# Retention attention by chunks of 64 positions on four array quarters, for the units of the last two batch groups

## The chip, the cores and the metric

One Trainium2 chip, one core. The time is device microseconds of one execution, the median of several; lower is better. Everything is float32 on the array.

## The reference

```python
def _attn_ref(q, k, v):                    # each (8, 8, 576, 64): batch, heads, positions, head_dim
    scores = (1 / sqrt(64)) * q @ k^T
    gamma = 1.0 - 2.0 ** (-5.0 - arange(H))
    Dmat = where(rel >= 0, gamma ** rel, 0)         # rel = query position - key position
    return (scores * Dmat) @ v

def _moe_ref(x, w1, w2, w3, w_out):        # x: (4608, 512), w1, w2: (512, 1024), w3: (1024, 1024), w_out: (1024, 512)
    return (((x @ w1) * (x @ w2)) @ w3) @ w_out

def reference(...):
    x = attention.transpose(0, 2, 1, 3).reshape(4608, 512)
    return _moe_ref(x, ...)
```

The decay factors as gamma^i * gamma^-j, so the kernel scales q rows by gamma^i / 8 and v rows by gamma^-j, masks the scores with a triangle of ones, and carries a state: the sum of k^T v over all earlier positions.

## The kernel before

**Attention in units.** Two batches at a time (four such pairs, i) and five chunks of the 576 positions (c): a unit g = 5 i + c, 20 in all. The first chunk of a pair has 64 positions, the other four have 128. A unit does, for two batches and eight heads:

- `score(g)` (line 233): k times q, 16 matmuls with 64 contraction rows and 128 output rows; DVE multiplies the four banks with the triangle into `pm` (line 236).
- `state(g)` (line 255): adds k^T v of the unit to the PSUM bank `st`; ACT copies it to `sb` (line 259) for the next unit. The last chunk of a pair has none.
- `pv_state(g)` (line 274): `sb` times q, 16 matmuls of 64 x 64, one on each quarter of the array in turn, into two banks `xps`.
- `pv(g)` (line 299): v times `pm`, added to the same banks; ACT copies them to `xT` (line 306), the token blocks.

Each f32 matmul shows as two records in the profile, each a weight load and a matmul.

**Two phases.** Up to about 366 us the program converts the weights, multiplies w3 and w_out together, and handles the first half of the tokens with one level of Strassen's scheme (`up`, `down`). From there on (units 10 to 19, `for g in range(2 * NC, G)`), tokens go in four groups with two levels of Strassen's scheme in the first product. One group is 17 items, done in order by `work(n)` from the list `todo`:

- 14 items `up2` (line 1028): seven small products each, with weight forms `ra` that are fetched from HBM by `next_forms` (line 939) into a ring of three slots. An `up2` takes PSUM tiles `p1` and `p5` from the pool `acc` and `p6` from `seed`. Its last product (`rest`: `A22`, `-T4`) is put off into the next item by way of `behind` and run by `finish()`. Sums lie on DVE (lines 1038, 1040), POOL (`more`, line 1033) and ACT (lines 1042 to 1057); `multiply()` makes the gated product `ab` on DVE (line 1003).
- 3 items `down` (line 637): seven products of 128 x 256 over `ab`, results to `ot`, stored by ACT's queue.

`token_forms(gr)` (line 948) makes a group's sums on POOL from `xT`: `E` and its fourth form `E4` (first-level sums of both token blocks) and `T`, `U` (second level).

**Order around a unit.** The order is written out by hand, each engine running its instructions in program order. `dealt` says how many items go to each unit. Between the items, `scale_blocks` (POOL) and `front_blocks` (DVE transposes) get q and k of the next unit ready, `front` (transposes on TensorE) k of units 11 to 13, `scale` (ACT) its v. The lists `aside`, `beside` and `loads` hold small steps that an item takes up at fixed points. Then, between two items and in one go: `pv(g)`, in a group's last unit (13, 16, 19: `ready`) `finish()` and `multiply()`, then the loads for g + 2 on POOL's queue, `state(g + 1)`, `score(g + 1)`:

```python
        pv(g)()
        if g in ready:
            finish()
            multiply()
        if g + 2 < G:
            load(g + 2, "v", nc.gpsimd)
            ...
        if g + 1 < G:
            state(g + 1)
            score(g + 1)
```

[...] In the second phase they are one for `st`, five for `acc`, two for `seed` (`open_second`).

Of the kernel before, what the change touches and what calls it, by code (L numbers as in the profile page):

```python
# [8 lines left out]
F32 = mybir.dt.float32  # L9
# [5 lines left out]
PSUM = bass.MemoryType.PSUM  # L15
# [4 lines left out]
def kernel(  # L20
# [30 lines left out]
    starts = [0] + [short + c * P for c in range(NC - 1)]  # L51
    G = NB2 * NC
    NB = 3
    TB = S // NB
# [23 lines left out]
    open_attention(att_part)  # L78
    st_ps = ctx.enter_context(tc.tile_pool(name="st_ps", bufs=1, space=PSUM))
    acc_part = ExitStack()  # L80
    acc = acc_part.enter_context(tc.tile_pool(name="acc", bufs=7, space=PSUM))

# [3 lines left out]

    def load(g, names, engine=nc.sync):
        i, c = divmod(g, NC)
        sz = sizes[c]
        src = {"k": k, "q": q, "v": v}  # L90
        for nm in names:
            t = pools["ld"].tile([P, 2 * H, D], F32, tag="ld_" + nm, name="ld_" + nm)
            engine.dma_start(
                t[:sz], src[nm][2 * i:2 * i + 2, :, starts[c]:starts[c] + sz, :].rearrange("b h p d -> p (b h) d"))
            live[nm, g] = t
# [181 lines left out]

    def pv(g):

        if ("xps", g) not in live:  # L280
            pv_state(g)
        i, c = divmod(g, NC)
        sz = sizes[c]
        live["x", g] = True
        vs, pm, banks = live["v", g], live["pm", g], live["xps", g]

        parts = []
        for n in range(NB):
            lo, hi = max(starts[c], n * TB), min(starts[c] + sz, (n + 1) * TB)
            if lo < hi:  # L290
                m = i * NB + n
                if ("xT", m) not in live:
                    live["xT", m] = xps[m % 4 == 3].tile([P, NP, 2, TB], F32, tag="xT", name="xT")
                parts.append((live["xT", m], lo - n * TB, lo - starts[c], hi - lo))
        for m, (b, n) in enumerate(bank_order):
            for r in range(2):
                for half in range(2):
                    p, j = 2 * r + n, half ^ r
                    nc.tensor.matmul(banks[r][heads[half], b, n, :sz], vs[:sz, b * H + 2 * p + j, :],  # L299
                                     pm[:sz, b, j, p, :sz], start=(c == 0 and m == 0), stop=True,  # L300
                                     skip_group_check=True)

        def evict():
            for x, to, fr, n in parts:
                for r in range(2):
                    nc.scalar.copy(
                        x[:, 2 * r:2 * r + 2, :, to:to + n].rearrange("p n b s -> p b n s"),
                        banks[r][:, :, :, fr:fr + n])

        return evict  # L310

    blocks = [(("A", r, f), None) for f in range(2) for r in range(2)]
# [309 lines left out]
    def down(x, y, then=None, last=False):  # L625
# [34 lines left out]

        C11, C12, C21, C22 = (0, 0), (0, 1), (1, 0), (1, 1)
        product(1, "A11", "B11")
        first = ot[:, 0, 0]
# [4 lines left out]
        if second:  # L668
            store()
            finish()  # L670
        product(7, "S3", "T3")
        if second:
# [8 lines left out]
        nc.vector.tensor_add(ot[:, 0, 1], ps[6], first)  # L681
        nc.scalar.copy(ot[:, 0, 0], ps[2])
        early = second or last or g >= 2 * NC - 1
        if early:
# [8 lines left out]
        if second:  # L693
            store()
        product(3, "S4", "B22", on=5)
        while aside and not early:
# [10 lines left out]
    def store():  # L707
        while stores:

            nc.scalar.dma_start(*stores.pop(0))  # L710
# [210 lines left out]
    def open_second():  # L921
        nonlocal acc
        flush()
        acc_part.close()
        acc = ctx.enter_context(tc.tile_pool(name="acc", bufs=5, space=PSUM, reuse_waits="tile"))
        pools["seed"] = ctx.enter_context(tc.tile_pool(name="seed", bufs=2, space=PSUM, reuse_waits="tile"))
        ra = wp.tile([P, 32 * P], F32, tag="wA1", name="ra")
        cs = wp.tile([P, 2, 4, 2, TB], F32, tag="wS1", name="cc")
        ring.extend([ra[:, :FORM], ra[:, FORM:2 * FORM]])
        free.extend(cs[:, j] for j in range(2))  # L930
        live["first"] = [ra[:, 2 * FORM + j * DM // 2:2 * FORM + (j + 1) * DM // 2] for j in range(2)]
        for _ in range(2):
            next_forms(nc.sync)
# [8 lines left out]
    def token_forms(gr):  # L942
# [13 lines left out]
        sums += [(T[:, s, 2], x[s][:, 2:, 0], T[:, s, 1]) for s in range(2)]  # L956
        for args in sums:
            tt(*args)
        tt(b12, b22, b12)
# [14 lines left out]
        if gr:  # L974
            rest()
        tt(T[:, 1, :, 0], T[:, 1, :, 1], T[:, 1, :, 0])
        for k in (slice(0, 2), 2):
# [13 lines left out]
    def finish():  # L991
        while behind:
            behind.pop(0)()
# [14 lines left out]
    def up2(gr, n):  # L1008
# [26 lines left out]
        def plus(ps, j, with_add=None):  # L1035
# [5 lines left out]
            else:  # L1041
                nc.scalar.copy(c[:, j], ps)

        p1 = acc.tile([P, 2, TB], F32, tag="acc", name="up")
        product(p1, "A11", "B11", True)
# [4 lines left out]
        product(p5, "S1", "T1", True)  # L1050
        nc.scalar.copy(c[:, 3], p5)  # L1051
        finish()
        next_forms()
        if loads:
# [9 lines left out]
        product(p1, "A12", "B21")  # L1064
        plus(p1, 0, add)
        product(p5, "S4", "B22")
        if add is not None:
# [11 lines left out]
        if aside:  # L1079
            aside.pop(0)()  # L1080

        def rest():
# [108 lines left out]
    load_blocks(g + 1, "q")  # L1191
    state(g)
    score(g)
    add_group(0)
    dealt = [3, 4, 4, 3, 3, 7, 7, 3, 7, 7]
    for g in range(2 * NC, G):
        n = dealt[g - 2 * NC]
        if g + 1 < G:
            beside.extend(lambda j=j: scale(g + 1, "v", range(j, j + H // 2)) for j in (0, H // 2))
            tail = min(n, 4) - 3  # L1200
# [4 lines left out]
            for nm in "qk":  # L1205
                blocks_in = nm == "q" or g + 1 not in whole
                if blocks_in:
                    aside.append(lambda nm=nm: front_blocks(g + 1, nm))
                work(1)
                while aside:  # L1210
                    aside.pop(0)()
                if not blocks_in:
                    while loads:
                        loads.pop(0)()
                    front(g + 1, "k")
                if g + 2 < G and not (nm == "k" and g + 2 in whole):
                    load_blocks(g + 2, nm)
            work(tail)
            for left in (loads, beside):
                while left:  # L1220
                    left.pop(0)()
        else:
            work(n)
        pv(g)()
        if g in ready:
            finish()
            multiply()
        if g + 2 < G:
            load(g + 2, "v", nc.gpsimd)
            if (g + 2) % NC != NC - 1:  # L1230
                loads.append(lambda g=g: load(g + 2, "k", nc.gpsimd))
        if g + 1 < G:
            state(g + 1)
            score(g + 1)
        if g in ready:
            add_group(ready[g])
        if g == G - 1:
            token_forms(ready[g])
    g = G
# [44 lines left out]
```

## Time and profile before

| | |
|---|---|
| median of 3 runs | 850.87 us (846.77 to 853.91) |
| the profiled execution's own time | 850.68 us |
| its span, first to last instruction | 848.9 us |
| granted TensorE clock, mean | 0.989 |
| PE busy | 819.3 us (97%), 6085 matmul records |
| DVE, ACT, POOL busy | 541.2, 283.2, 325.6 us |

PE is TensorE's matmuls, PEld its weight loads, DVE VectorE, ACT ScalarE, POOL GpSimd, SP SyncE's queue. A row of the timeline has the start, the length from the first start to the last end, engine, line, what is written and read, the array rows and columns used, the moving operand's shape and the number of records; in brackets the idle time ahead of it and what ended it. The ends of matmuls are modelled and overlap the next ones, so a rate is read from the starts of successive rows.

### The profile page before, as it was taken

What the parts mean: (1) busy time and instruction counts of PE and PEld (TensorE: products, weight loads), DVE (VectorE), ACT (ScalarE), POOL (GpSimd) and SP (SyncE); (2) the same over time, 40 slices, a digit from 0 to 9 for tenths busy, and PEclk for the clock granted to TensorE, in tenths of its full rate; (3) what the DMA queues carried; (4) which work ended last, traced back from release to release, by engine and by line L of the source; (5) the groups of instructions that cost most, each with busy time, mean ns of one, the idle gap of its engine ahead of it and who ended that gap; (6) DMA issues with size and microseconds to landing.
All of it is one profiled execution on the core that took longest, in us unless ns stands there. A gap on an engine that the chain in (4) does not pass through costs nothing.

```text
span 848.9 us, 15774 instructions
## 1 busy us (share of the span) xinstructions
PE 819.3 (97%) x6085; PEld 738.1 (87%) x6085; DVE 541.2 (64%) x887; ACT 283.2 (33%) x581; POOL 325.6 (38%) x330
## 2 busy tenths in 40 slices
PE   7899999999999999979998999999999999999998
PEld 6889999644989998869998889998899998899987
DVE  4899999991644477615657644759735768446653
ACT  4777556670111101033343024342034331033300
POOL 1100010001104181395545935556916468445500
PEclk8999999999999999999999999999999999999999
DMA  9995454436046487979786147787275452245401
GB/s 193 217 224 128 77 150 125 126 98 112 1 98 125 75 220 251 307 209 220 190 229 167 44 93 228 201 238 177 58 156 183 140 208 69 77 148 189 159 25 51
DMA packets 201291, 126.96 MB, mean 150 GB/s; under 512 B 161272, under 2 KB 183032, under 8 KB 201216
## 3 DMA queue, kind: packets, MB, share of 16 engines
q1 hardware_dynamic: 170944, 50.14, 29.1%
q0 software_dynamic: 11776, 63.71, 23.0%
q10 hardware_dynamic: 18496, 12.10, 5.3%
q8 instruction: 48, 0.79, 0.4%
q14 instruction: 27, 0.22, 0.1%
HBM read 103.62 MB, written 22.28 MB: 148 GB/s over the span
## 4 chain that ended last, share of the span: by engine, by line
PE 79%; DMA 7%; DVE 7%; issue 3%; SPq 2%; ACT 1%; POOL 0%; ACTq 0%; DVEq 0%; POOLq 0%
PE po L637 24%; PE up L1028 15%; PE up L524 13%; PE seed L1028 11%; PE ps L477 6%; DMA ld_v<-in_v_dram 3%; PE xps L299 3%; PE sc L233 3%; DMA ra<-kept 2%; PE xps L274 1%; SPq L171 1%; DVE c L529 1%; DVE ab L1003 1%; DMA bl_q<-in_q_dram 1%; PE st L255 1%
## 5 line engine op out<-in xcount | busy, mean ns | idle before, releaser
L637 PE MATMUL po<-w3o,ab 128*128 128x256 f32 x552 | 125.0, 381 | 1.4 <-DVE ot L641 0.5
L637 PEld LDWEIGHTS po<-w3o,ab 128*128 128x128 f32 x552 | 103.9, 190 | 17.4 <-DVE ot L641 1.2
L1033 POOL TENSOR_TENSOR cc<-cc 128x384 f32<-128x384 f32 x112 | 109.3, 1001 | 4.1 <-ACT cc L1051 2.4
L1040 DVE TENSOR_TENSOR cc<-seed,cc 128x384 f32<-128x384 f32 x88 | 48.7, 553 | 72.9 <-PE seed L1028 68.5
L181 POOL TENSOR_TENSOR bl_q<-bl_q,gqs 128x512 f32<-128x512 f32 (+1 forms) x30 | 30.8, 1048 | 127.7 <-DMA bl_q<-in_q_dram 91.8
L939 POOL DMA_DIRECT2D ra<-kept x54 | 30.6, 567 | 124.1 <-PE seed L1028 103.3
L1028 PE MATMUL up<-xT,ra 128*128 128x192 f32 x384 | 74.2, 330 | 0.6 <-DMA ra<-kept 0.6
L1040 DVE TENSOR_TENSOR cc<-up,cc 128x384 f32<-128x384 f32 x88 | 48.4, 550 | 36.8 <-PE up L1028 31.5
L524 PE MATMUL up<-xT,wA 128*128 128x192 f32 x384 | 70.4, 327 | 0.0
L529 DVE TENSOR_TENSOR c<-up,c 128x384 f32<-128x384 f32 x80 | 44.0, 550 | 38.9 <-PE up L524 38.3
L1028 PEld LDWEIGHTS up<-xT,ra 128*128 128x128 f32 x384 | 64.4, 192 | 2.0 <-DMA ra<-kept 0.9
L236 DVE TENSOR_TENSOR pm<-sc,mask 128x512 f32<-128x512 f32 (+1 forms) x80 | 45.4, 626 | 32.1 <-PE sc L233 32.0
L637 PE MATMUL po<-wB,forms 128*128 128x256 f32 x288 | 65.2, 379 | 0.5 <-DVE forms L611 0.5
L524 PEld LDWEIGHTS up<-xT,wA 128*128 128x128 f32 x384 | 63.4, 190 | 1.1 <-issue 0.5
L637 PEld LDWEIGHTS po<-wB,forms 128*128 128x128 f32 x288 | 54.6, 190 | 8.2 <-PE po L637 0.8
L1047 ACT COPY seed<-up 128x384 f32<-128x384 f32 x56 | 25.9, 463 | 100.1 <-PE up L1028 46.6
L1028 PE MATMUL seed<-e,ra 128*128 128x192 f32 x256 | 52.9, 337 | 5.2 <-DVE cc L1040 2.9
L1028 PE MATMUL up<-ra 128*128 128x192 f32 x288 | 55.1, 328 | 1.9 <-DMA ra<-kept 1.9
L477 PE MATMUL ps<-wo,w3T 128*128 128x512 f32 x128 | 55.1, 592 | 0.0
L204 POOL TENSOR_TENSOR ld_v<-ld_v,gk 128x1024 f32<-128x1024 f32 (+1 forms) x9 | 17.1, 1899 | 90.5 <-DMA ld_v<-in_v_dram 90.5
L679 DVE TENSOR_TENSOR ab<-ab,forms 128x512 f32<-128x512 f32 x17 | 17.1, 1008 | 53.3 <-PE po L637 53.3
L1028 PEld LDWEIGHTS seed<-e,ra 128*128 128x128 f32 x256 | 43.7, 194 | 7.8 <-DVE cc L1040 3.6
(127 smaller groups left out, 1597.2 us busy)
## 6 DMA issues: line engine op xcount, KB each, us to landing
ra<-kept POOLq DMA_DIRECT2D x54, 896.0 KB, 5.0
raw<-in_moe_w_dram SPq DMA_DIRECT2D x72, 128.0 KB, 3.0
bl_q<-in_q_dram SPq DMA_DIRECT2D x216, 32.0 KB, 3.2
out_dram<-ot ACTq DMA_DIRECT2D x54, 128.0 KB, 2.3
bl_k<-in_k_dram SPq DMA_DIRECT2D x136, 32.0 KB, 2.4
raw<-in_moe_w_dram SPq DMA_DIRECT2D x16, 256.0 KB, 6.0
ld_k<-in_k_dram SPq DMA_DIRECT2D x8, 512.0 KB, 5.9
raw<-in_moe_w_out_dram SPq DMA_DIRECT2D x32, 128.0 KB, 2.7
```

Source lines behind the costliest of these rows:

```text
L181: nc.gpsimd.tensor_tensor(out=part, in0=part, in1=gqs[:, :, n0:n0 + n].unsqueeze(3).to_broadcast([P, NP, n, BL]), op=ALU.mult)
L233: nc.tensor.matmul(sc[j][:sz, p, :sz], kT[hs, b, p, :sz], qT[hs, b, p, :sz], start=True, stop=True)
L236: nc.vector.tensor_mul(pm[:sz, b, j, :, :sz], sc[j][:sz, :, :sz], mask[:sz, :sz].unsqueeze(1).to_broadcast([sz, NP, sz]))
L477: nc.tensor.matmul(ps, live["w3T", ft][:, g, :], live["wo"][:, g, :], start=(g == 0), stop=(g == KF - 1))
L524: nc.tensor.matmul(ps[:, w, :], a[:, w, r, :], b[:, r, :], start=(new and w == r == 0), stop=(w == r == 1), skip_group_check=True)
L529: nc.vector.tensor_add(c[:, to], ps, c[:, sb])
L637: nc.tensor.matmul(ps[nm], a[A][:, f, :], live["W"][B][:, f, :], start=(f == 0 and not on), stop=(f == NP - 1), skip_group_check=True)
L939: engine.dma_start(ring[n % 3], kept[n % 14 // 7][nm])
L1028: nc.tensor.matmul(ps[:, w, :], weight_of(slot, a, w), B[b], start=(new and w == 0), stop=True, skip_group_check=True)
L1033: nc.gpsimd.tensor_tensor(out=o, in0=o, in1=i, op=ALU.add)
L1040: nc.vector.tensor_add(c[:, j], ps, with_add[:, j])
L1047: nc.scalar.copy(p6, p1)
```

## The change

For the units of the second phase, 10 to 19 (the change's own words say nine; the code treats all ten so), a chunk of 128 positions is computed as two of 64:

- `score2`: only the two diagonal 64 x 64 blocks of the scores, 32 matmuls of 64 x 64 with 64 moving columns, one on each quarter of the array in turn; two banks instead of four, and two DVE instructions for the mask.
- `state2`: k^T v of the two halves, each in a bank of its own (`st` is now two banks), so 32 matmuls on four quarters; the state ahead of each half is built by `ahead_of` (an ACT copy or a DVE add), with a copy `odd` of the second bank. The last chunk of a pair gets a state for its second half too, for which half a chunk of k is loaded.
- `state_half` and `pv_half`: state and value products, each half of a chunk from its own state and its own scores. The value products come in two halves; a tiny ACT copy `hand` lies between them, since the second adds into places that other array rows wrote.
- These are no longer done between items. A list `plan` holds pieces, `begin_item()` takes one entry at the start of an item, and `here()` runs a piece at two points of an `up2` (after `p5`'s copy; after the sum of `p1`) and of a `down` (at its start; after `finish()`). The item behind a unit's own ones does `first_half` and `second_half` with the evictions and loads, the one after it scores and sums of the next unit.
- `acc` has four buffers in the second phase instead of five, to make room for `st`.
- The third weight form is fetched at `open_second` on SP's queue, with the first two; `token_forms` makes the sums of `T` behind those of `E`; v is scaled in four steps instead of two; `dealt` is changed, and one more item lies between the last unit and its token forms.

The diff, cut to its core:

```diff
-    def load(g, names, engine=nc.sync):
+    def load(g, names, engine=nc.sync, chunks=2):
-        sz = sizes[c]
+        sz = min(sizes[c], chunks * CS)
...
+    def score2(g):
+        n = (sizes[g % NC] // CS)
+        kT, qT = live["kT", g], live["qT", g]
+        sc = [acc.tile([P, 2, NP, CS], F32, tag="acc", name="sc") for j in range(2)]
+        for b in range(2):
+            for p in range(NP):
+                for s in range(n):
+                    at_s = slice(s * CS, (s + 1) * CS)
+                    for j, hs in enumerate(heads):
+                        nc.tensor.matmul(sc[j][heads[s], b, p, :], kT[hs, b, p, at_s], qT[hs, b, p, at_s],
+                                         start=True, stop=True)
+        sz = n * CS
+        pm = live["pm", g] = live["pm2"]
+        for j in range(2):
+            nc.vector.tensor_mul(
+                pm[:sz, j].rearrange("p b m x -> p (b m) x"), sc[j][:sz].rearrange("p b m x -> p (b m) x"),
+                mask[:sz, :CS].unsqueeze(1).to_broadcast([sz, 2 * NP, CS]))
+
+    def state2(g):
...
+        n = 1 if c == NC - 1 else (sizes[g % NC] // CS)
...
+                for s in range(n):
+                    for j, hs in enumerate(heads):
+                        h = b * H + 2 * p + j
+                        nc.tensor.matmul(st[hs, s, b, p, :], kn[heads[s], h, :], vs[heads[s], h, :],
+                                         start=(c == s and b == 0 and p == 0), stop=(c >= NC - 2),
+                                         skip_group_check=True)
+
+        def ahead_of(g, s, odd):
+            sb = live["sb", g, s] = pools["fr"].tile([P, 2, NP, D], F32, tag="sb", name="sb")
+            if odd is None:
+                nc.scalar.copy(sb, st[:, 0])
+            else:
+                nc.vector.tensor_add(sb, st[:, 0], odd)
+
+        if n == 2 or c:
+            ahead_of(g, 1, live.get(("odd", g)))
+        if c < NC - 1:
+            odd = None
+            if n == 2:
+                odd = live["odd", g + 1] = live["odd2"]
+                nc.scalar.copy(odd, st[:, 1])
+            live["next", g] = lambda: ahead_of(g + 1, 0, odd)
...
+    def state_half(g):
+        qT = live["qT", g]
+        banks = live["xps", g] = [acc.tile([P, 2, 2, P], F32, tag="acc", name="xps") for r in range(2)]
+        if g % NC:
+            for s in range(2):
+                at_s = slice(s * CS, (s + 1) * CS)
+                for m, (b, n) in enumerate(bank_order):
+                    for r, j in ((0, 0), (0, 1), (1, 0), (1, 1)):
+                        p = 2 * r + n
+                        nc.tensor.matmul(banks[r][heads[j ^ r], b, n, at_s], live["sb", g, s][heads[j], b, p, :],
+                                         qT[heads[j], b, p, at_s], start=(m == 0 and s == 0), stop=False,
+                                         skip_group_check=True)
+
+    def pv_half(g, second):
...
+        for m, (b, n) in enumerate(bank_order):
+            for r0, s in ((0, 0), (0, 1), (1, 0), (1, 1)):
+                j, r = s ^ second, r0 ^ second
+                half, p = j ^ r, 2 * r + n
+                if s < (sizes[g % NC] // CS):
+                    nc.tensor.matmul(
+                        banks[r][heads[half], b, n, s * CS:(s + 1) * CS], vs[heads[s], b * H + 2 * p + j, :],
+                        pm[heads[s], j, b, p, :], start=(c == 0 and m == 0), stop=True, skip_group_check=True)
+        if not second:
+            last = (heads[1 if c == 0 else 0], 1, 1, slice(sz - 1, sz))
+            nc.scalar.copy(hand[last[0]], banks[1][last])
...
+    def begin_item():
+        if plan:
+            att.extend(plan.pop(0))
+
+    def here(n=1):
+        while att and n:
+            att.pop(0)()
+            n -= 1
...
-        acc = ctx.enter_context(tc.tile_pool(name="acc", bufs=5, space=PSUM, reuse_waits="tile"))
+        st_ps = ctx.enter_context(tc.tile_pool(name="st_ps2", bufs=1, space=PSUM, reuse_waits="tile"))
+        acc = ctx.enter_context(tc.tile_pool(name="acc", bufs=4, space=PSUM, reuse_waits="tile"))
...
-        for _ in range(2):
+        for _ in range(3):
             next_forms(nc.sync)
...
-        for args in sums:
-            tt(*args)
         tt(b12, b22, b12)
         tt(E[:, 1], b12, b11, ALU.add)
         tt(E[:, 0], b22, E[:, 1])
...
         if gr:
             rest()
+        for args in sums:
+            tt(*args)
...
         nc.scalar.copy(c[:, 3], p5)
+        here()
         finish()
-        next_forms()
+        if sent[0] < steps[0] + 2:
+            next_forms()
...
         plus(p1, 0, add)
+        here()
         product(p5, "S4", "B22")
...
-    dealt = [3, 4, 4, 3, 3, 7, 7, 3, 7, 7]
+    dealt = [3, 5, 3, 3, 3, 8, 6, 3, 8, 6]
...
+        def half_and_loads(g=g):
+            second_half(g)
+            if g + 2 < G:
+                def late():
+                    load(g + 2, "v", nc.gpsimd)
+                if g + 2 in whole:
+                    load(g + 2, "k", nc.gpsimd)
+                else:
+                    late()
+                    late = lambda: load(g + 2, "k", nc.gpsimd, 1 if (g + 2) % NC == NC - 1 else 2)
+                loads.append(late)
+
+        def next_scores(g=g):
+            for left in (beside, loads):
+                while left:
+                    left.pop(0)()
+            scores_and_sums(g + 1)
+
         if g in ready:
+            first_half(g)
             finish()
             multiply()
-        if g + 2 < G:
-            load(g + 2, "v", nc.gpsimd)
-            if (g + 2) % NC != NC - 1:
-                loads.append(lambda g=g: load(g + 2, "k", nc.gpsimd))
+            plan.append([half_and_loads])
+            add_group(ready[g])
+        else:
+            plan.append([lambda g=g: first_half(g), half_and_loads])
         if g + 1 < G:
-            state(g + 1)
-            score(g + 1)
-        if g in ready:
-            add_group(ready[g])
-        if g == G - 1:
-            token_forms(ready[g])
+            plan.append([next_scores])
+    work(1)
+    token_forms(3)
```

## The prediction

> **What bounds the kernel now.** I read the page first (spans, engine shares, the chain that ended last), then busy time by stage, then the timeline of TensorE around the attention units.
>
> ```profile
> span 848.9 us, 15774 instructions
> PE 819.3 (97%) x6085; PEld 738.1 (87%) x6085; DVE 541.2 (64%) x887; ACT 283.2 (33%) x581; POOL 325.6 (38%) x330
> ...
> PE 79%; DMA 7%; DVE 7%; issue 3%; SPq 2%; ACT 1%; POOL 0%; ACTq 0%; DVEq 0%; POOLq 0%
> ```
>
> TensorE (PE) is busy for 97% of the span and holds 79% of the chain. The stages (columns: stretch, its length, busy us of PE, weight loads, DVE, ACT and POOL with instructions, granted clock, DMA share, GB/s):
>
> ```profile
> 366.60:390.00 23.40, 17.74 (x86) 16.84 (x86) 5.16 (x9) 7.46 (x19) 18.41 (x19) 0.85 0.72 175
> ...
> 470.00:705.00 235.00, 231.74 (x1754) 216.26 (x1752) 144.07 (x233) 67.00 (x161) 138.98 (x139) 1.00 0.58 159
> ```
>
> The second phase (366.6 to the end) is the one the change rewrites. Over its long middle TensorE is busy for 231.7 of 235 us and no other engine for over 62%: time is saved there only by giving TensorE less, or by closing its last gaps. The exception is the ramp at 366.6, with 5.7 us of idle and a clock of 0.85. One unit of attention in the middle, then one of 64 positions, then the gaps that matter:
>
> ```profile
> 438.32 0.81 PE L1028 MATMUL seed<-xT,ra 128*128 128x192 f32 x4
> 439.06 1.10 PE L274 MATMUL xps<-qT,sb 64*64 64x128 f32 x32
> 440.10 1.97 PE L299 MATMUL xps<-pm,ld_v 128*64 128x128 f32 x32
> 441.89 1.10 PE L255 MATMUL st<-ld_v,ld_k 128*64 128x64 f32 x32
> 442.93 2.06 PE L233 MATMUL sc<-qT,kT 64*128 64x128 f32 x32
> 444.91 0.92 PE L1028 MATMUL up<-ra 128*128 128x192 f32 x4
> 445.67 0.65 PE L1028 MATMUL up<-u,ra 128*128 128x192 f32 x3
> ```
> ```profile
> 250.30 1.15 PE L299 MATMUL xps<-pm,ld_v 64*64 64x64 f32 x32
> 251.38 1.15 PE L255 MATMUL st<-ld_v,ld_k 128*64 128x64 f32 x32
> 252.46 2.06 PE L233 MATMUL sc<-qT,kT 64*128 64x128 f32 x32
> ```
> ```profile
> 383.16 1.20 PE L1028 MATMUL up<-ra 128*128 128x192 f32 x4 [1.91 <-DMA ra<-kept]
> ...
> 462.73 0.92 PE L1028 MATMUL seed<-e,ra 128*128 128x192 f32 x4 [0.78 <-DVE cc L1040]
> 465.37 3.62 PE L233 MATMUL sc<-qT,kT 64*128 64x128 f32 x32 [1.72 <-DVE kT L190]
> ...
> 546.22 2.05 PE L233 MATMUL sc<-qT,kT 64*128 64x128 f32 x30 [0.68 <-DVE cc L1040]
> ...
> 705.67 5.34 PE L637 MATMUL po<-w3o,ab 128*128 128x256 f32 x24
> 711.48 1.75 PE L637 MATMUL po<-wB,forms 128*128 128x256 f32 x7 [0.47 <-DVE forms L611]
> ```
>
> Every f32 matmul is two records (16 matmuls of a unit's state show as x32). Starts matter here, not durations: the unit takes TensorE from 439.06 to 444.91, 5.85 us.
>
> **Prices.** Successive rows give 162.5 ns for a 192-wide record and 216 ns for a 256-wide one: 53.5 ns for 64 columns. From the starts of single records: L274 starts four quarters 6.7 ns apart and repeats every 109 ns (128 columns); L255, two halves of the columns, repeats every 58.4 ns (64 columns); L233 and L299 repeat every 105 ns (two, 128 columns). So a group costs the columns of one member plus 2 to 5 ns, with two or four members. No row has four quarters at 64 columns. If only columns count, such a group is 58.4 ns, 14.6 ns a record (a weight load and its matmul, "a pair").
>
> Switches: the record group ahead of the attention takes 743 ns for 650 (+0.09), the one after 754 (+0.10), and a run of 16 groups by itself takes 1.08 for 0.93 us (+0.15, the row at 250.30). A piece alone among large matmuls thus pays 0.34 us.
>
> [...] The trace has 6.7 ns between tiles and 27 on the mean of L274[...]. [...] In this trace its sequencer's semaphore records stand 16 to 20 pairs ahead of the array (at 627.80 one for L255, whose run begins at 628.76, 18 pairs later), even 48 pairs into a stream at 29 ns. So instructions arrive at 29 ns a pair or faster; how much faster no row tells.
>
> **The change part by part.** [...]
>
> 1. *Array work.* A unit of 128 positions now has 16 groups each of scores, state, state product and value product at 58.4 ns: 64 x 58.4 = 3.74 us, plus three pieces (scores with sums, first half, second half) x 0.34 = 1.02; 4.76 together. Before: 5.85 + 0.09 + 0.10 = 6.04. Six such units (11 to 13, 16 to 18) save 1.28 each: -7.7. Units 14 and 19 had no state: 5.1 (L274 1.03, L299 1.90, L233 1.99, switches 0.2), now 4.76: -0.3 each. Units 10 and 15 have one chunk, which fills two quarters: 48 x 58.4 ns as before, but in three pieces: about +0.4 each. Sum: -7.5.
>
> 2. *Waits of the scores.* They now run a whole item (4.55 us) or more behind the transposes and slots they need. The 1.72 at 465.37, the run at 545.05 (3.14 for 1.99, +1.15) and that of unit 19 (2.60 for 1.99, +0.6) go: -3.4. What is late next is the item's own matmul, and that is the following steps.
>
> 3. *Units 13, 16 and 19*, where finish() follows. At 462.73 the product of finish() waits for DVE, which is behind with transposes and products, although 2.75 us of attention lay before it. The first half is 64 + 32 records' worth, 24 groups = 1.4 us + 0.34: some 0.9 us less cover, all of it given back as a longer wait: +2.7. The scores that stood between finish() and the next down item move away; at 705.67, without that cover, 24 records took 5.81 us for 5.18 and 0.47 followed, 1.1 us; before, units 13 and 16 lost 0.12 and 0.67: +1.4.
>
> 4. *Ramp.* The third weight form goes out on SP with the first two instead of on POOL at 377.6, so the 1.91 at 383.16 goes with part of the half-speed clock behind it (384.16 to 387.55 took 3.4 us for 1.95). The token sums that moved behind E let the first item start at about 364.7, not 369.7, but POOL works without a pause to the last form at 377.68, and the second item waits for that either way; the clock after that longer wait is slow for some 1.7 us. Counting from 377.7: now 11.8 us to the end of the third item, then about 9.3: -2.5.
>
> 5. *Slots.* acc has four buffers for five. An item holds two, a piece takes two more, so the second of these is the slot that the item before freed last: DVE's add for p5, done 1.33 us into the next item (650.30: 651.63), where the piece begins at 1.30. With the semaphore some 0.1 us in 15 pieces: +1.5. Bounds: 0, and 0.4 each, +6.
>
> 6. *Beside TensorE.* Score masks fall from four DVE instructions of 0.63 us to two; the state takes one or two adds of about that size and an ACT copy of 0.59 more, and the tiny copy "hand" makes the second half wait for the first, with 1.9 us of products between (1.7 in a down item). ACT (67 of 235 us) and DVE (144 of 235) hide it; uncovered it would be 1 us a unit. POOL's load of v waits at the second half, and `more` queues behind it for its 1.1 us, as it did between items before. k for units 14 and 19 is two loads of half a chunk, beside 0.58 DMA share: 0. Quartered v scaling is the same ACT work: 0.
>
> Sum: -7.5 - 3.4 + 2.7 + 1.4 - 2.5 + 1.5 = -7.8. The profiled execution took 850.68 (span 848.9 and 1.8 around it), 0.2 below the median of 850.87: 850.7 - 7.8 = 842.9, say 843.
>
> **Rivals.**
> *Instructions arrive too slowly (slower).* A piece of 128 pairs drains a lead of about 18 pairs at 14.6 ns, then runs at what the sequencer delivers. At 28 ns: (110 + 78) x 13.4 ns = 2.5 us for the scores and first-half pieces of each of eight units, 20 us: 843 + 20 = 863. For it: [...] nothing in this trace faster than 27 a record over a run. Against it: the lead does not shrink at 29. It costs 1.5 us for each ns above 14.6, so the gain is gone at about 20 ns.
> *Waits inside the items eat the gain.* The slot at its upper bound (+4.5), v arriving late at ACT, which has its copies for the item queued behind: 848 to 853. For it: DVE ends within 0.1 us of need. Against: DVE's add ends 1.32 to 1.33 us into each of the items that start at 641.20, 645.75 and 650.30; it does not scatter.
> *Pieces also fill gaps.* If finish() is not awaited longer and the losses in second items (637.36: 1.90 for 1.30; 515.80: 2.12) vanish: 843 - 5 = 838. Against: DVE's backlog is not in the moved part.
>
> **How the numbers follow.** Forecast 0.38 (840 to 847), gaps filled 0.13, waits 0.16, slow delivery 0.33 (mostly above 859, less if between 18 and 25 ns). A per cent, 8.5 us, is about what a measurement of this kernel can tell. Faster by more: 0.13 and 0.15 of the forecast, 0.28; slower by more: 0.28; the rest 0.44. Range: 837 to 864.
>
> **What would show it.** Steps 1 and delivery: a scores piece takes about 2.2 us on TensorE (3.4 or more means slow delivery), and group starts 58 ns apart. Step 2: no L233-like row waits for kT. Step 3: the product after the first half of units 13 and 16 waits 1.5 us and more for DVE. Step 4: no wait for kept forms before 390. Step 5: waits for DVE ahead of a piece's second tile, in sum about 1.5 us. Wrong if TensorE's attention falls by under 4 us, or if waits of items exceed 6 us.

## The result, and the profile after

The changed kernel takes 875.27 us (median of 4, 869.22 to 877.44), the kernel before 852.39 in the same comparison: a ratio of 1.027 (1.0221 to 1.032). It is slower by 23 us where 843 was forecast; the slower rival said 863. The profiled execution took 876.38. In the ratios below, the kernel before is that of the same comparison on the same chip. Some executions run slower, one of them at a much lower clock (the change with two forms: 941.27 us at 0.846, for 871.33 at 0.978); the ratios leave them out, and of two variants whose profiled execution was such a one (third form alone, and the change with two forms) only the times are used for sizes.

The page of the kernel after: its span, its engines and the chain that ended last:

```profile
span 874.7 us, 17886 instructions
PE 824.5 (94%) x7109; PEld 739.1 (84%) x7109; DVE 536.5 (61%) x880; ACT 285.1 (33%) x593; POOL 318.3 (36%) x327
...
PE 72%; issue 8%; DVE 8%; DMA 5%; POOL 3%; SPq 3%; ACT 1%; ACTq 0%; DVEq 0%; POOLq 0%
```

Lines of the kernel after: 328 `score2`, 350 `state2`, 382 `state_half`, 395 `pv_half`, 752 a `down`, 1157 the products of an `up2`, 1162 `more`, 1167 and 1169 DVE's sums, 1132 `multiply()`, 1068 `next_forms`.

The busy time by stage, same columns as before:

```profile
470.00:705.00 235.00, 218.51 (x2276) 200.95 (x2268) 131.46 (x213) 64.26 (x162) 121.76 (x124) 0.96 0.56 146
```

TensorE, busy for 231.7 of these 235 us before, now is for 218.5, at a clock of 0.96 instead of 1.00. So the middle stage, where TensorE was nearly always busy, has gained idle time. What ended it, from the waits of TensorE in the second phase (columns: sum, times, longest, in us):

```profile
PE seed L1157 <- DVE cc L1169: 14.5, 6, 4.3
PE seed L1157 <- issue: 7.1, 2, 3.9
PE up L1157 <- DMA ra<-kept: 6.1, 2, 3.7
...
PE st L350 <- issue: 1.7, 2, 1.1
```

The same view of before has 2.9 us for the first of these, 2.5 for the third, and no "issue" at all.

The attention itself did get cheaper. Adding up TensorE's records of the second phase from start to start, the attention takes 45.3 us for 54.5, the switches of array mode 2.7 for 0.9: -7.4 together. But the rest of the phase grew by 34 us: the longer stops 37.4 for 15.0, and the slow clock behind them, with small gaps, 20.4 for 8.3. These sums are of single executions, and the start of the second phase scatters by some us between executions with the same code ahead of it (its first `seed` row stands at 365.25 in the kernel before and at 374.84 in the one with four `acc` buffers).

### The profile page after: what moved, and what is told of

Its sections match the earlier page's. It is cut to its first block, busy times and chain, and to the rows that moved or that the text cites. A ratio compares the mean times of both kernels' runs of the same rounds, so it can differ in the third digit from the quotient of the medians.

```text
span 874.7 us, 17886 instructions
## 1 busy us (share of the span) xinstructions
PE 824.5 (94%) x7109; PEld 739.1 (84%) x7109; DVE 536.5 (61%) x880; ACT 285.1 (33%) x593; POOL 318.3 (36%) x327
## 4 chain that ended last, share of the span: by engine, by line
PE 72%; issue 8%; DVE 8%; DMA 5%; POOL 3%; SPq 3%; ACT 1%; ACTq 0%; DVEq 0%; POOLq 0%
PE po L752 22%; PE up L1157 13%; PE up L639 12%; PE seed L1157 11%; PE ps L592 6%; POOL cc L1162 2%; DMA ra<-kept 2%; DMA out_dram<-ot 2%; PE xps L310 2%; PE sc L234 1%; DVE c L644 1%; SPq L172 1%; PE sc L328 1%; PE st L350 1%; PE xps L395 1%
## 5 line engine op out<-in xcount | busy, mean ns | idle before, releaser
L752 PE MATMUL po<-w3o,ab 128*128 128x256 f32 x552 | 128.1, 387 | 2.6 <-ACT ot L784 1.6
L1169 DVE TENSOR_TENSOR cc<-seed,cc 128x384 f32<-128x384 f32 x88 | 48.6, 552 | 88.9 <-PE seed L1157 71.5
L1157 PE MATMUL up<-xT,ra 128*128 128x192 f32 x384 | 76.9, 335 | 4.8 <-DMA ra<-kept 2.4
L1169 DVE TENSOR_TENSOR cc<-up,cc 128x384 f32<-128x384 f32 x88 | 48.4, 550 | 43.4 <-PE up L1157 36.7
L1157 PE MATMUL seed<-e,ra 128*128 128x192 f32 x256 | 56.6, 354 | 19.3 <-DVE cc L1169 14.5
L1157 PEld LDWEIGHTS up<-xT,ra 128*128 128x128 f32 x384 | 66.2, 196 | 6.2 <-issue 3.0
L1157 PE MATMUL up<-ra 128*128 128x192 f32 x288 | 57.5, 337 | 3.7 <-DMA ra<-kept 3.7
L1157 PEld LDWEIGHTS up<-ra 128*128 128x128 f32 x288 | 50.5, 198 | 4.0 <-issue 3.9
L592 PEld LDWEIGHTS ps<-wo,w3T 128*128 128x128 f32 x128 | 24.3, 190 | 30.1 <-issue 29.7
```

The lines of the kernel that those rows point to most:

```text
L592: nc.tensor.matmul(ps, live["w3T", ft][:, g, :], live["wo"][:, g, :], start=(g == 0), stop=(g == KF - 1))
L752: nc.tensor.matmul(ps[nm], a[A][:, f, :], live["W"][B][:, f, :], start=(f == 0 and not on), stop=(f == NP - 1), skip_group_check=True)
L1157: nc.tensor.matmul(ps[:, w, :], weight_of(slot, a, w), B[b], start=(new and w == 0), stop=True, skip_group_check=True)
L1169: nc.vector.tensor_add(c[:, j], ps, with_add[:, j])
```

## The experiments

The expectations speak of four theories. A: attention was moved away from places where it covered a late DVE. B: TensorE's instructions arrive too slowly. C: the three forms fetched at once delay what stands behind them at the ramp. D: the PSUM slots of `acc` are too few.

### Does an instruction stream this dense run dry?

The two largest new stops of the middle lie behind the scores and sums, and end with "issue": nothing that the profile shows was waited for. From TensorE's timeline of the kernel after:

```profile
454.01 1.10 PE L328 MATMUL sc<-qT,kT 64*64 64x64 f32 x59 [0.26 <-DVE cc L1169]
...
454.96 1.15 PE L350 MATMUL st<-ld_v,ld_k 64*64 64x64 f32 x63
456.03 0.59 PE L1157 MATMUL seed<-u,ra 128*128 128x192 f32 x2
459.91 2.08 PE L1157 MATMUL seed<-u,ra 128*128 128x192 f32 x6 [3.28 <-issue]
```

The pieces themselves run near the forecast rate of 14.6 ns a pair: 64 scores pairs in 0.98 us (649.91 to 650.90), 15 ns a pair. The array stops behind them, two large matmuls into the item. A burst put into the kernel before, once, at the start of the second phase, shows the supply by itself:

```diff
+            tb = [pools["seed"].tile([P, 2, TB], F32, tag="seed", name="burst") for _ in range(2)]
+            for _ in range(128):
+                for x, y in ((0, 0), (1, 1), (0, 1), (1, 0)):
+                    nc.tensor.matmul(tb[x][heads[y], 0, :64], ident[heads[x], heads[x]],
+                                     live["w3o"][heads[x], 0, :64], start=True, stop=True)
```

(1,024 pairs on four quarters, written into the two buffers of `seed`; of this kernel only the times are used, not the output.)

> The kernel before with 512 further matmuls of 64 x 64 with 64 columns, on the four quarters in turn, ahead of the first up2 item (1024 pairs, 2048 PE instructions, results not used). If instructions come at 14.6 ns a pair for as long as wanted, they take 15 us. Theory B, fetching: the first few hundred instructions run at about 15 ns a pair, then the run stops at each chunk of 256 instructions until the next fetch of 16 KB is in; with the 4 to 5 us seen in the changed kernel between a fetch's start and the next matmul, 8 chunks take 25 to 40 us.

It took 877.51 us in one execution, and the burst 27.4 us of it, where 15 would do by the forecast's estimate of 14.6 ns a pair. TensorE's timeline:

```profile
378.01 2.61 PE L1021 MATMUL burst<-w3o,ident 64*64 64x64 f32 x155
382.04 2.09 PE L1021 MATMUL burst<-w3o,ident 64*64 64x64 f32 x128 [1.41 <-issue]
...
393.50 2.09 PE L1021 MATMUL burst<-w3o,ident 64*64 64x64 f32 x128 [1.36 <-issue]
396.95 2.09 PE L1021 MATMUL burst<-w3o,ident 64*64 64x64 f32 x128 [1.36 <-issue]
```

The array runs exactly 128 pairs, 256 instructions, at about 15 ns a pair, and then stands still. In the steady part such a block comes every 3.45 us (393.50, 396.95): 27 ns a pair on the mean. The page's queue q8, kind "instruction", moves 0.79 MB in 48 packets before and 0.92 MB in 56 after: 16,384 bytes each. The change adds 1,024 pairs, 2,048 instructions, and eight packets: 256 instructions a packet. That is the size of the blocks in which the burst ran: after 155 pairs and then after every 128 the array stopped, as if about one block were ahead.

In the kernel after, the last 128 pairs ahead of the stop at 456 are 2 large ones, 64 sums and 62 scores: the block began at about 454.0 and was used up in 2.4 us. The next was there 5.9 us after that start, not 3.45. (Between 450 and 462 us a weight form of 896 KB, 512 KB of v and 256 KB of k are fetched besides; that these slow the fetch of instructions is possible, and was not tried apart.) Before, 128 pairs of a full unit lasted 5.85 us.

Three runs of the changed kernel move the instructions against the blocks. The first puts the sums at the second point of the scores' item; the second (`one_piece`) into an item of their own; the third only adds half a block (64 small pairs) at the start of the phase.

```diff
-            plan.append([next_scores])
+            plan.append([next_scores, lambda g=g: state2(g + 1)])
```

> The changed kernel with each scores piece split: scores at the first point of an item, sums of the state at its second, so that no run has more than 128 PE instructions there. Theory B: issue idle falls from 8.8 us to under 3, with the slow clock behind it, 863 to 868 in all. Theory A: waits for DVE stay at 17 us, and if fetching were not the cause of the issue idle, 874 to 876.

```diff
             plan.append([next_scores])
+            plan.append([lambda g=g: state2(g + 1)])
```

> The changed kernel with scores and sums in items of their own, one behind the other, so that no item holds more than 64 pairs of scores or sums (halves as they were). Theory B (a chunk of 256 PE instructions has to last 3.5 to 5 us or the array waits for the next one): an item of 64 small and 28 large pairs lasts 5.6 us, so the idle put down to issue falls under 3 us, and 864 to 868 in all. Otherwise 873 to 877.

```diff
+            tb = [acc.tile([P, 2, TB], F32, tag="acc", name="shift") for _ in range(2)]
+            for _ in range(8):
+                for x, y in ((0, 0), (1, 1), (0, 1), (1, 0)):
+                    nc.tensor.matmul(tb[x][heads[y], 0, :64], ident[heads[x], heads[x]],
+                                     live["w3o"][heads[x], 0, :64], start=True, stop=True)
```

> The changed kernel with 32 matmuls of 64 x 64 (64 pairs, 128 instructions, half a chunk) ahead of the first up2 item, where TensorE waits anyway; results not used. Theory B: the fetch boundaries move by half a chunk, so the long stops behind the scores of units 13 and 18 (3.3 and 3.9 us) go or become stops inside a piece, and others appear elsewhere. If they come from anything in the order of the work, they stay behind units 13 and 18.

Within an item: 875.22 us, ratio 1.024 (1.0174 to 1.0306), no gain. In two items: 865.65, ratio 1.0125 (1.0037 to 1.0213). Shifted by half a block: 865.55 in one execution, below the fastest of the four of the changed kernel. In the first the stops for issue are 5.5 us, for 8.8 in the kernel after, so part of them went and yet the time did not fall; what took that gain was not found. TensorE's timeline shows one stop that stayed:

```profile
454.26 1.15 PE L328 MATMUL sc<-qT,kT 64*64 64x64 f32 x62 [0.25 <-DVE cc L1169]
...
457.49 1.04 PE L350 MATMUL st<-ld_v,ld_k 64*64 64x64 f32 x54
461.19 0.59 PE L350 MATMUL st<-ld_v,ld_k 64*64 64x64 f32 x10 [2.66 <-issue]
```

62 scores, 12 large matmuls and 54 sums are 128 pairs again, now used up in 4.1 us, while the next block came 6.9 us after the start of this one.

The trace says the same without any theory. Count TensorE's records from the program's start, weight loads, matmuls and semaphore instructions together. The four stops for issue in the kernel after come behind 6,080, 6,848, 7,616 and 11,457 of them: 3, 3 and 15 times 256 apart, to one. With the sums at the second point the two long ones come behind 7,616 and 11,457 again, though sums of the state stand there now and not an item's matmuls. And so in every run: all 31 stops for issue of over 0.2 us behind 366 us, in ten kernels, the burst among them, leave the same rest of 192 or 193 when their count is divided by 256. The stop belongs to a place in the instruction stream, not to a piece of work.

In the shifted kernel the two waits for issue in the second phase are short:

```profile
PE up L1162 <- issue: 0.4, 1, 0.4
...
PE st L350 <- issue: 0.2, 1, 0.2
```

Both cures give about 9.6 us, and have little in common but where the dense pieces lie against the blocks. By the ratios the second gives 12 us, and by its profile it pays some 3 us of that for ten more switches of array mode. The stops for issue of the kernel after add up to 8.8 us, and the clock is low behind the long ones (0.50 from 459.9 to 461.8, where six records take 1.87 us for 0.98). Of all that was tried on the changed kernel, moving dense pieces and blocks against each other moved its time most.

### The edits at the side

The third form on SP and the sums of T behind those of E were put into the kernel before, together and the first alone, and taken out of the changed kernel, both in the version with sums in an item of their own (`one_piece_no_side`) and the first alone:

```diff
-        for _ in range(2):
+        for _ in range(3):
             next_forms(nc.sync)
...
-        for args in sums:
-            tt(*args)
         tt(b12, b22, b12)
...
-        tt(T[:, 1, :, 0], T[:, 1, :, 1], T[:, 1, :, 0])
+        for args in sums:
+            tt(*args)
```

> The kernel before with the two side edits of the change alone: three weight forms fetched at the start on SP instead of two, and the sums of T behind those of E. My prediction: 848 (2.5 us faster). Theory C: the first form lands later (a wait of some 2.5 us ahead of the first item) and POOL waits for q blocks behind it on SP's queue (a product of the second or third item waits 3 to 5 us for DVE), 854 to 858.

> The kernel before with three forms fetched at the start on SP and nothing else. My prediction's step 4: the wait of 1.9 us for the third form goes, 850 to 852. If the larger fetch delays the first form and the q blocks behind it: 854 to 857, and the sums' order then is innocent of most of the 3.5 us.

> The changed kernel with two forms fetched at the start and the third by POOL in the first item, as before. Theory C: the wait for the first form goes (2.4 us) and q blocks land earlier; the third form is waited for by some 2 us; 869 to 873. Without C: 875 to 877.

> As one_piece, and without the side edits (two forms at the start, sums of T ahead of E as before). From the 3.5 us that the side edits cost in the kernel before: 860 to 865.

In the kernel before both cost 857.57 us, ratio 1.0041 (1.0016 to 1.0066); the third form alone a ratio of 1.0057 (1.0019 to 1.0095). Taken out of the changed kernel, the third form alone left 872.58 (three executions), ratio 1.0212 (1.0149 to 1.0274), no difference from 875.27 that can be told. Both taken out, with the sums apart: 859.8, ratio 1.0091 (1.006 to 1.0123), 5.8 less than with them by the medians and 2.9 by the ratios, whose intervals overlap: in the changed kernel a gain is likely, not shown. In the kernel before the cost is shown, 3.5 us by the ratio (1.4 to 5.6), and the forecast of -2.5 has the wrong sign. The third form alone costs as much there as both, as far as the intervals tell; more on how the two divide these runs don't tell.

One mechanism shows at the ramp. POOL's timeline, kernel before and then kernel after:

```profile
378.26 2.08 POOL L181 TENSOR_TENSOR bl_q<-bl_q,gqs 128x512 f32<-128x512 f32 x2
...
380.90 1.95 POOL L1033 TENSOR_TENSOR cc<-cc 128x384 f32<-128x384 f32 x2
```
```profile
381.44 2.06 POOL L182 TENSOR_TENSOR bl_q<-bl_q,gqs 128x512 f32<-128x512 f32 x2 [4.83 <-DMA bl_q<-in_q_dram]
...
384.08 1.95 POOL L1162 TENSOR_TENSOR cc<-cc 128x384 f32<-128x384 f32 x2
```

And DVE's and TensorE's, kernel after:

```profile
385.11 0.56 DVE L1169 TENSOR_TENSOR cc<-seed,cc 128x384 f32<-128x384 f32 x1 [5.57 <-POOL cc L1162]
```
```profile
385.73 1.65 PE L1157 MATMUL seed<-e,ra 128*128 128x192 f32 x4 [4.25 <-DVE cc L1169]
```

The blocks of q stand behind the third form on SP's queue. POOL has to wait for them and scales them 3 us later than before, ahead of `more`; DVE waits for `more`, and TensorE stands for 4.25 us, until 385.73, for DVE, with a clock of 0.50 behind that (385.7 to 388.5). From the TensorE row that starts with POOL's last form to the end of the third item, where transposes follow, it is 11.8 us before (377.73 to 389.50), 15.3 after (376.66 to 391.94) and 15.2 in the kernel before with both edits (376.80 to 391.98): 3.5 us more, as the times say. The third form did come in time: it was not what ended last.

### The places, the dealing and the fifth buffer

The old pieces in the new places, with all else as in the change (`full_in_items`); the same with old dealing and without the side edits (`full_in_items_plain`; an `acc` of five in both); and the quarters in the old place, between the items:

> The attention of the kernel before (128 positions, state in one bank, acc with five buffers) in the new places: value products at the first point of the item behind a unit's own, its eviction at the second, state and the scores of the first batch at the first point of the item after that, the scores of the second batch at its second point; dealt, forms and token sums as in the changed kernel. Theory A: as slow as the changed kernel apart from issue: 862 to 872, waits for DVE 12 us or more. Theory B: issue idle near 0, and if B were the main cause 850 to 856.

> Attention of 128 positions in the new places as in full_in_items, but with the items dealt as before and without the side edits (two forms at the start, sums of T ahead of E): only the place of the pieces differs from the kernel before, acc has five buffers. Theory A, the place alone costs: 862 to 868, waits for DVE 10 us or more. If place costs nothing and the 21 us of full_in_items came from the dealing and the side edits: 850 to 856.

> The quartered attention of the changed kernel in the old place: both halves, loads, scores and sums in one go between two items, items dealt as before the change; acc has four buffers, three forms at the start and the sums of T behind E as in the changed kernel. Theory A (attention moved away from the places where it covered a late DVE; about 13 us of the loss): the waits for DVE fall back from 17 us to about 5, total 848 to 855. Theory B (a run of some 256 PE instructions in 2 us empties the instruction buffer and the next fetch takes some 5 us): the runs are now longer, so the idle time put down to issue stays at 9 us or grows, total 860 to 868. Theory C (the three forms fetched at once and the late q blocks behind them, ramp): the 7 us at the ramp stay under both.

Full pieces: 873.26, ratio 1.0227 (1.0157 to 1.0296), and plain 858.56, ratio 1.006 (1.0035 to 1.0084): the place alone costs the old pieces some 5 us, between the two forecasts. Quarters between the items, with the old dealing: 875.68, ratio 1.0232 (1.015 to 1.0313); there the tiny copy `hand` also stops the array ten times for 2.7 us, and issue costs 5.5 us at the scores. So the old place is no cure: a unit in one go is 256 pairs in some 4 us of work. What the place does apart from `hand` and issue, that run can't tell.

The dealing, put into the kernel before, taken out of the changed one, and out of the changed one with sums apart and without side edits:

```diff
-    dealt = [3, 4, 4, 3, 3, 7, 7, 3, 7, 7]
+    dealt = [3, 5, 3, 3, 3, 8, 6, 3, 8, 6]
```

> The kernel before with the items dealt as in the change (3, 5, 3, 3, 3, 8, 6, 3, 8, 6), nothing else. If the dealing alone carries part of the loss (attention then stands behind other items than those where DVE is late): 858 to 863, more waits for DVE than the 5 us of before. Otherwise 852 to 855.

> The changed kernel with the items dealt to the units as before (3, 4, 4, 3, 3, 7, 7, 3, 7, 7). Theory A: the pieces stand nearer to the items where DVE is late; some of the waits go, 866 to 872. Theory B: no change of issue idle beyond where the bursts fall against the fetches, 873 to 878.

> As one_piece_no_side, with the items dealt as before the change. If place and dealing set where DVE's lateness shows: 853 to 857, since it then differs from full_in_items_plain (858.6) by the array's 8 us less and acc's four buffers. If the dealing is without effect: 859 to 862.

865.65, ratio 1.0148 (1.0086 to 1.021); 873.76, ratio 1.0232 (1.0155 to 1.0308); 859.5, ratio 1.009 (1.0057 to 1.0123). The new dealing harms the old pieces in the old place by about 12 us and makes no difference to the new ones, each of which comes an item later. Added to the side edits it would account for the 873 of the full pieces (858.6 + 12.1 + 3.5 = 874.2), though it was measured in the old place only; the changed kernel does not get its time back without it.

The fifth buffer, taken from the kernel before:

```diff
-        acc = ctx.enter_context(tc.tile_pool(name="acc", bufs=5, space=PSUM, reuse_waits="tile"))
+        acc = ctx.enter_context(tc.tile_pool(name="acc", bufs=4, space=PSUM, reuse_waits="tile"))
```

> The kernel before with four acc buffers instead of five in the second phase, nothing else. My prediction's step 5: 852 to 853. Theory D (the slots are the main loss): scores and the products of down items wait for DVE's and ACT's reads, 860 or more.

859.21, ratio 1.0065 (1.004 to 1.0091): 5.4 us. Its profile does not put that where it was forecast. The second phase is as long as before (480.1 us for 480.3 from its first `seed` record); it starts 9.6 us later, at 374.84. Ahead of that a DVE sum lies beside POOL's and is long. DVE's timeline, then POOL's, of this run:

```profile
358.57 6.68 DVE L679 TENSOR_TENSOR ab<-ab,forms 128x512 f32<-128x512 f32 x1 [4.79 <-PE po L637]
```
```profile
357.05 1.94 POOL L948 TENSOR_TENSOR xT<-xT 128x384 f32<-128x384 f32 x2
358.96 1.93 POOL L948 TENSOR_TENSOR ra<-xT 128x384 f32<-128x384 f32 x2
360.86 3.84 POOL L948 TENSOR_TENSOR ra<-xT,ra 128x384 f32<-128x384 f32 x4
```

One DVE sum of two SBUF operands took 6.68 us, until 0.5 us behind the end of POOL's row at 364.70; in the kernel before it took 1.62. That part of the program is the same in both, so this may be chance of this execution; the comparison of 20 executions with 38 says that the buffer costs something, and where it does in most executions is open. In the kernel after, the waits for a slot, DVE ahead of a scores tile, are 0.5 us in all.

### What remains in the new places

The best version with the new pieces (sums apart, no side edits) still lies 6.8 us above before (7.8 by the ratio), although its attention with the switches takes 4.4 us less than before (not 7.4: ten more pieces pay for switches). Between 395 and 735 us its stops come to 16.4 us against 6.2 before, and four of them, 9.0 us, stand in the kernel after too, within 0.02 us each (2.42, 2.16, 2.43, 1.98). One of them, in the kernel after, DVE's, POOL's and TensorE's timelines:

```profile
546.26 2.71 DVE L1132 TENSOR_TENSOR ab<-cc 128x384 f32<-128x384 f32 x1
548.89 1.23 DVE L191 STREAM_TRANSPOSE qT<-bl_q 128x1024 f32<-128x1024 f32 x1
```
```profile
546.58 1.96 POOL L1162 TENSOR_TENSOR cc<-cc 128x384 f32<-128x384 f32 x2
```
```profile
552.01 2.93 PE L1157 MATMUL seed<-e,ra 128*128 128x192 f32 x8 [2.42 <-DVE cc L1169]
```

The product of two SBUF tiles takes 2.71 us instead of the 0.5 of most of its sisters: it ends 0.43 us behind POOL's two sums, about its own length. It is not alone: of the run's 64 such products (L1132) eight take over 0.7 us (0.92 to 3.69), and each of these ends 0.41 to 0.43 us behind the end of a POOL operation beside it; the other 56 take 0.53 to 0.56. (DVE's record starts 0.3 us ahead of POOL's, and yet it is DVE's that is long.) DVE's sums with one PSUM operand (L1167, L1169) take 0.51 to 0.56 us, all 240 of them, of which 119 lie beside a POOL operation. The transposes queue up behind, then the sums that TensorE needs. Before, it was no better for DVE (the mean of these products is 833 ns in the middle stage, 771 after): but attention stood between, and the scores of that unit waited for 0.68 us only (546.22).

The new places are not needed for this: the dealing alone does it. The kernel before with the new dealing, its old pieces in the old place, stands just as long at the same product, behind the same slow DVE operation (DVE's, then TensorE's timeline of that run):

```profile
542.13 2.70 DVE L1003 TENSOR_TENSOR ab<-cc 128x384 f32<-128x384 f32 x1
```
```profile
547.88 2.22 PE L1028 MATMUL seed<-e,ra 128*128 128x192 f32 x8 [2.42 <-DVE cc L1040]
```

So it does at 674.27 (2.42), and at 573.60 it waits 2.48 for a weight form: from 395 to 735 us its stops are 17.0 us for 6.2, most of its 12 us. The new pieces with the old dealing (sums apart, no side edits) lack these two stops, but there the value products themselves wait for DVE instead, 1.95 and 0.70 us at 543.58 and 544.61, and the state products as long at 669.08 and 670.10. That is why the dealing matters to the old pieces and not to the new ones: as these rows read, in neither order does enough work lie ahead of the first matmul that waits for the late DVE.

## Why the prediction was wrong

The forecast was -7.8 us, the result +23. What failed is first that the sum put the delivery of instructions at nothing, against the rival that the prediction named; then the sign of step 4; then step 6, by which DVE's work is hidden; and `dealt`, which no step priced. The prediction's own sign of being wrong, waits of items over 6 us, is there: 14.5 us for DVE in one row of the waits.

The sizes, measured as a ladder from before to after: 853.0; all of the change but its side edits, with sums apart, 859.8 (+6.8); the side edits, 865.65 (+5.8); scores and sums in one piece, 875.3 (+9.6, from another chip's comparison). By the ratios the same three steps are +7.8, +2.9 and +12.4, so the order of the last two is firmer than their sizes.

- **Step 1, array work, -7.5: right.** -7.4 was measured; 16 groups of scores take 0.98 us with a part of the switch, where 0.93 without it was forecast.
- **The slower rival, instructions: the mean right, the form and price wrong, and the choice wrong.** It took a steady 28 ns a pair behind a lead of 18 pairs. Supply is 27 ns a pair on the mean, but in blocks: scores and sums take 2.07 us (649.91 to 651.98) where 2.2 was to clear the rival and 3.4 to prove it, and the stop comes behind them, in an item's matmul. The test chosen, the length of the piece, was blind to it. The sequencer's lead of "16 to 20 pairs" at 29 ns showed how far ahead it stood, not how fast that is refilled. It costs about 9.6 us by the cures, not 20: the array stopped for issue at four places in ten units, where the end of a block fell in or just behind a dense piece.
- **Step 2, waits of the scores, -3.4: right by itself.** No scores row waits for kT, and the rows at 454.01 and 565.16 wait 0.26 and 0.24 for DVE.
- **Step 3, units 13, 16 and 19, +2.7: right in sum, too narrow in place.** Units 16 and 19 wait 2.16 and 1.98 for 0.79 and 0; unit 13's 0.78 is gone: +2.6. The down items behind them lose 2.7 us for 1.9, +0.8 where +1.4 was forecast. But cover went in ordinary items also, which step 6 put at nothing, since ACT and DVE would "hide it": the stops of 2.42, 2.43 and 2.38 at 552.01, 687.95 and 419.95, for one of 0.68 before, add 6.6. The weights' fetch that ended last once for 3.66 us (0.62 was the longest such wait behind the ramp before) was in no step. The argument is the one that step 3 made for three units; the new dealing alone brings stops like these four to the kernel before (2.42, 2.42, 1.73 and 2.48), and no step priced it.
- **Step 4, ramp, -2.5: wrong sign.** The working looked at the wait that ends (the form) and at POOL's sums, not at the q blocks behind the form on SP's queue. +3.5 at the ramp by the profiles, +3.5 in the kernel before by the times (1.4 to 5.6), 2.9 to 5.8 in the changed one.
- **Step 5, slots, +1.5: mis-sized or misplaced.** Its waits are 0.5 us; taking away the buffer alone costs 5.4 (3.4 to 7.8), near the bound of 6, and in the one profile elsewhere than argued.
- **Slow clock.** No step but 4 priced the slow clock behind a stop. The mean clock fell from 0.989 to 0.977.

That the terms add up is a reading of the ladder, not shown. What stays open: where the missing fifth buffer loses its time; how the side edits divide; why the first split of the pieces gained nothing; what of the remaining 7 us is lost to the buffer and what to DVE's missing cover.

## What to carry to other kernels

Where a piece replaces large matmuls by many small ones, count its instructions against the refill: 256 of them (128 pairs) that last less than the 3.45 us seen here, or the 5.9 and 6.9 us seen at two stops, can stop the engine where the block ends, often after the piece and not in it; so spread such pieces between long matmuls, and look for "issue" in the waits. When a transfer is moved to another queue, write down all that stands behind it there and who waits for that. Before work that covers a late engine is moved, look for every place where it covers one, and count the order of the items as a part of the move: DVE, busy for 64% here, caught up in attention's time, and TensorE's largest row of waits for it was 2.9 us before that time was moved and 14.5 after.

## What the hardware showed that was not expected

In the burst TensorE ran in blocks of 256 instructions, as if about one block were ahead: 128 pairs at about 15 ns, then 1.36 us of nothing, every 3.45 us; and in ten kernels every such stop fell on the same one of 256 places of the instruction stream, or the next. And a DVE operation on two SBUF operands lasted until a row of POOL operations had ended: 6.68 us, in the one execution seen, for one that took 1.62 in the kernel before, its end 0.5 us behind that of POOL's row; in the kernel after all eight products of over 0.7 us ended 0.41 to 0.43 us behind a POOL operation.
